# Attention followed by a squared-ReLU MLP: the second half of the attention written out in order, its side work dealt by units, high parts of early weights on GpSimd

## The chip, the core and the metric

One core of a Trainium2 chip runs the whole program. The metric is the device time of one execution in microseconds; lower is better. Engines are named as the profile names them: PE (TensorE), DVE (VectorE), ACT (ScalarE), POOL (GpSimd) and SP, whose queue issues the DMAs.

## The reference

```python
# q, k, v: (4, 8, 576, 64); bias: (576, 576) per head from positions by a small MLP
scores = q @ k.T / sqrt(64) + bias
attn = exp(scores - max); attn /= attn.sum(-1)
x = (attn @ v) as (2304, 512)
h = x @ w_in            # w_in (512, 2048)
out = max(h, 0)**2 @ w_out   # w_out (2048, 512)
```

The bias depends on head and positions alone, so it is computed once for the four batches.

## The kernel before

Attention works in units `(b, hp, ic)`: a batch, a pair of heads, and a chunk of 128 query rows; chunk 4 is the tail of 64 rows, in which both heads share one tile. `units` has 80 of them. The first 40 (`NA = 40`) run over both first batches, chunk by chunk, while the bias is computed into `area`. The last 40 run over batches 2 and 3, head pair by head pair, five chunks each; a head pair's part of `area` is free once its units are done.

A unit takes three steps. `scores(u)` (L420) multiplies q and k on PE (L438) into one score buffer `sp` in PSUM; DVE evicts it per head with bias and maximum (L444, `negm`), ACT takes the exponential and the row sums (L449); for a tail unit POOL copies 64 columns (L452). `transposes(u)` (L485) turns p on PE (L494, L497), ACT copies it to `pt` (L495, L498). `values(u)` (L501) multiplies with v on PE (L512) and DVE copies the result to `xT` (L517). The loop (L663) emits `scores(s)`, `transposes(s-2)`, `values(s-3)` in step s. After the last chunk of a head pair, `normalise` (L454) inverts the row sums on DVE (L457, L458), splits them in three bf16 parts on POOL (L461, L463), and turns them by one product (L466) that ACT copies (L468); `scale_x` (L471) spreads them on PE (L480) and multiplies `xT` on DVE (L483).

Beside the units runs side work for the MLP, which computes in split precision and by a seven-product block scheme. `scan_w` (L211) finds the largest weight of the 16 raw tiles of w_in, which arrive by `load_w` in two buffers tagged `stage`; `scale_w` (L214) makes a power of two of it. `split_in` (L224) makes eight early operands of w_in (`early`): `lead_w` (L171) takes absolute values on ACT (L176) and rebuilds float32 words from int64 halves in four DVE instructions (L179 to L182), POOL makes sums of blocks (L241 to L243), ACT writes the high part in f16 (L230), DVE the low part (L231). `x_largest` and `set_scale` scale x, `split_x` (L623) splits batch 0's x: sums on POOL (L635), high parts on ACT (L637), low parts on DVE (L638). The operands' places in `area` are `wdst` and `xs_at`; an operand can only be written where the bias is no longer read.

The order in each engine's queue is Tile's planner's: it takes program order as priority, places instructions by estimated times, and keeps the order written only for those passed to `keep_in_program_order` (score products after the first, scans, the first ACT instruction of early operands). Which step emits which side work is fixed by constants: `SC = 41` and `SN = 12` for scans, `WB`, `WS`, `LW` and the freeing of `area` for `when`, `XS`, `X1`, `XB` for x.

k and q of all eight first groups lie in one pool `kqa` (L91). At `s == NA` it is closed and a pool `kqb` with three buffers opened (L666, L667), into which `load_k` and `load_q` bring the second half's.

The MLP (L965 on) is written in order under `manual_schedule`: 40 items of `products` (L862), sums, squares, a split of g in high and low parts (L898, L899) and `down` (L954). Its first statements fetch two tiles of w_out (`first_outs`) and make their parts with `lead` and `high_out` (L789, L790), and run POOL's `sums_x` (L830) for batch 1.

## Time and profile before

| | us |
|---|---|
| median of 3 runs | 762.73 (762.21 to 762.75) |
| the profiled execution | 763.08 |
| its span, first to last instruction | 761.1 |
| PE busy | 719.4 (95%) |
| DVE busy | 554.9 (73%) |
| ACT busy | 476.3 (63%) |
| POOL busy | 170.3 (22%) |

The span is the time between the first and the last instruction of the profiled execution; 2.0 us lie around it. Busy time of PE holds the model's latency of a matmul, so back-to-back products overlap in their rows: what a product costs is read from one start to the next.

### The profile page before, as it was taken

Reading aid. Unit: us, or ns where it says so; the run is one execution under the profiler, and the core shown is the slowest. Engines: PE = TensorE matmul, PEld = TensorE weight load, DVE = VectorE, ACT = ScalarE, POOL = GpSimd, SP = SyncE. Lnnn points to the kernel's source line nnn. Section 1 sums busy time; section 2 is a strip of 40 time slices with the busy share of each in tenths; the row PEclk is TensorE's granted clock in tenths of the full one; section 3 lists DMA queues with packets and bytes.
Section 4 is the critical chain, followed back from the end, with each engine's and each line's share of the span. In section 5 each row is a group of like instructions: output and inputs, shape, how many; then the busy total and the mean of one; then the engine's idle time right before and its main releaser. Section 6 shows DMA issues by size and latency. Waiting matters only on the chain.

```text
span 761.1 us, 18188 instructions
## 1 busy us (share of the span) xinstructions
PE 719.4 (95%) x7382; PEld 579.0 (76%) x7382; DVE 554.9 (73%) x1178; ACT 476.3 (63%) x946; POOL 170.3 (22%) x281
## 2 busy tenths in 40 slices
PE   6889999999989999979998999999999999999992
PEld 6867878777757777657776888888888888888881
DVE  6689878775666677897498887878558775568651
ACT  4367787877647677878676675676566554455220
POOL 1474333331210023352114321312101112000000
PEclk7599999999999999999999999999999999999997
DMA  7620000000487622200350333332018332533100
GB/s 204 194 81 18 5 15 2 2 3 4 115 297 229 211 62 89 88 6 25 122 197 13 141 139 152 111 131 79 1 62 311 109 129 98 208 111 112 56 2 28
DMA packets 31607, 75.33 MB, mean 99 GB/s; under 512 B 5540, under 2 KB 13732, under 8 KB 30500
## 3 DMA queue, kind: packets, MB, share of 16 engines
q1 hardware_dynamic: 31524, 74.17, 28.5%
q8 instruction: 58, 0.95, 0.5%
q14 instruction: 25, 0.20, 0.1%
HBM read 55.81 MB, written 18.35 MB: 97 GB/s over the span
## 4 chain that ended last, share of the span: by engine, by line
PE 78%; DVE 11%; ACT 3%; issue 2%; DMA 2%; POOL 1%; SPq 0%; ACTq 0%; DVEq 0%
PE y L954 25%; PE ha L862 11%; PE px L512 9%; PE sp L438 9%; PE hb L862 8%; PE pp L494 7%; PE bb L386 4%; PE bb L405 2%; DVE t L444 2%; DMA stage<-in_w_in 2%; DVE mask L375 2%; PE pa L497 1%; ACT p L449 1%; DVE wa L181 1%; ACT pt L495 1%
## 5 line engine op out<-in xcount | busy, mean ns | idle before, releaser
L954 PE MATMUL y<-w,gh 128*128 128x512 f32 x576 | 183.1, 399 | 1.6 <-ACT gh L898 1.6
L862 PEld LDWEIGHTS <-area 128*128 128x128 f16 x1680 | 147.7, 98 | 25.5 <-issue 9.5
L449 ACT ACTIVATE p<-t,negm 128x576 f32<-128x576 f32 x144 | 111.1, 774 | 25.9 <-DVE negm L444 25.7
L444 DVE CUSTOM_DVE_ANT_0 t<-sp,area 128x576 f32<-128x576 f32 x144 | 103.9, 752 | 31.9 <-PE sp L438 26.9
L954 PEld LDWEIGHTS y<-w,gh 128*128 128x128 f32 x576 | 106.0, 190 | 23.3 <-ACT gh L898 2.3
L954 PE MATMUL y<-w,gl 128*128 128x512 f32 x288 | 113.9, 395 | 0.7 <-DVE gl L899 0.7
L438 PE MATMUL sp<-k,q 64*128 64x288 f32 (+1 forms) x640 | 103.0, 432 | 9.4 <-DVE negm L444 6.3
L495 ACT COPY pt<-pp 128x512 f32<-128x512 f32 x144 | 79.4, 582 | 35.4 <-PE pp L494 35.2
L512 PE MATMUL px<-pt,v 128*64 128x128 f32 (+1 forms) x1600 | 97.8, 269 | 2.8 <-DVE bt L392 1.2
L512 PEld LDWEIGHTS px<-pt,v 128*64 128x64 f32 x1600 | 80.0, 138 | 19.4 <-issue 7.6
L494 PE MATMUL pp<-ident,p 128*128 128x128 f32 x576 | 84.8, 284 | 1.6 <-ACT pt L495 1.2
L862 PE MATMUL ha<-area 128*128 128x256 f16 (+1 forms) x816 | 84.8, 260 | 0.7 <-DVE c L879 0.7
L438 PEld LDWEIGHTS sp<-k,q 64*128 64x128 f32 (+1 forms) x640 | 54.3, 177 | 31.4 <-issue 10.7
L494 PEld LDWEIGHTS pp<-ident,p 128*128 128x128 f32 x576 | 62.6, 143 | 19.2 <-issue 9.8
L397 POOL TENSOR_TENSOR area<-bt,bt 128x256 f32<-128x256 f32 x72 | 54.2, 775 | 73.2 <-DVE bt L392 73.2
L375 DVE TENSOR_TENSOR mask<-sdist,theta 128x1024 f16<-128x1024 f16 x81 | 57.2, 742 | 13.5 <-PE bb L405 7.3
L954 PEld LDWEIGHTS y<-w,gl 128*128 128x128 f32 x288 | 54.4, 189 | 13.9 <-DVE gl L899 1.9
L862 PE MATMUL hb<-area 128*128 128x256 f16 (+1 forms) x612 | 64.7, 260 | 0.0
L899 DVE TENSOR_TENSOR gl<-area,gh 128x512 fp32r<-128x512 f32 (+1 forms) x40 | 25.8, 668 | 29.8 <-ACT gh L898 28.1
L790 POOL TENSOR_TENSOR w<-wa,w 128x512 fp32r<-128x512 f32 x16 | 20.9, 1308 | 96.1 <-ACT w L789 96.1
L386 PEld LDWEIGHTS <-mask 128*128 128x128 f16 x1152 | 37.4, 100 | 4.8 <-issue 3.7
L386 PE MATMUL bb<-wmov,mask 128*128 128x64 f16 x1152 | 41.0, 197 | 0.0
(173 smaller groups left out, 980.3 us busy)
## 6 DMA issues: line engine op xcount, KB each, us to landing
stage<-in_w_in SPq DMA_DIRECT2D x24, 512.0 KB, 4.1
r<-in_w_out SPq DMA_DIRECT2D x16, 512.0 KB, 5.9
xs<-area SPq DMA_DIRECT2D x4, 1792.0 KB, 12.9
py<-o SPq DMA_DIRECT2D x12, 512.0 KB, 3.5
o<-py SPq DMA_DIRECT2D x12, 512.0 KB, 4.3
v<-in_v SPq DMA_DIRECT2D x16, 320.0 KB, 4.3
q<-in_q SPq DMA_DIRECT2D x32, 128.0 KB, 3.5
zw<-in_w_in SPq DMA_DIRECT2D x8, 512.0 KB, 3.6
```

The lines of the kernel that those rows point to most:

```text
L375: DVE.tensor_tensor(out=out, in0=win, in1=th, op=ALU.is_ge)
L386: PE.matmul(bb[:, 64 * (7 - r):64 * (8 - r)], lhsT=m[:, r], rhs=wmov[:, n], start=(n == 0), stop=(n == 1))
L397: POOL.tensor_tensor(out=dst, in0=tw, in1=sw, op=ALU.add)
L438: mm = PE.matmul(out_t[to, x, :HALF], lhsT=qt[rows, cols], rhs=kt[rows, k0:k0 + HALF], start=True, stop=True)
L444: DVE.tensor_tensor_reduce(out=t.rearrange("p (x n) -> p x n", x=2), in0=sp[:, :, :HALF], in1=bias.rearrange("p (x n) -> p x n", x=2), sca ...
L449: ACT.activation(out=p[:, S * n:S * n + S], in_=t, func=AF.Exp, bias=negm[:, n:n + 1], scale=-1.0, accum_out=sums[:, 2 * ic + n:2 * ic + n ...
L494: PE.transpose(pp[:, 128 * c:128 * c + 128], p[:, k0:k0 + 128], ident)
L495: ACT.copy(pt[:, 4 * h:4 * h + 4], pp.rearrange("p (c m) -> p c m", c=4))
L512: PE.matmul(px[64 * h:64 * h + 64, :w], lhsT=vt[:, c, h], rhs=src, start=(c == 0), stop=(c == 4))
L862: PE.matmul(h[:, s, :w], lhsT=a, rhs=x, start=(k == 0), stop=(k == 5))
L899: DVE.tensor_tensor(out=gl, in0=g, in1=gh.bitcast(F32), op=ALU.subtract)
L954: PE.matmul(y_t[n][k], lhsT=a[:, slot, o:o + 128], rhs=x, start=((n, P) in firsts and f == 0 and m == 0), stop=((n, P) in lasts and f == 1 ...
```

## The change

The loop over steps stops at the first half. The second half (s from 40 to 83) is one region under `manual_schedule`: each engine gets its instructions in the order in which they are emitted. A step emits the loads, the score products, the transposes, then in turns ACT's copies and the softmax of the two heads, then `fill(s)`, then `values(s-3)`.

Side work is kept as jobs: lists of stages, each with an engine, a price in microseconds and a function. Per step DVE gets room of 1.65 (2.5 in a tail step) and ACT of 0.45 (1.9); `fill` goes through the jobs in order and emits a stage when its time has come and its engine has room. A stage on another engine waits for the next step, except after PE and from DVE to POOL. Normalisations and scales go ahead of other jobs.

k and q of the first three groups lie in `kqa` with three buffers, which the second half uses again; those of the other five in `kqb`, closed at the end of the first half. The second half's first loads are emitted at s = 34 and 35. Raw tiles of w_in are fetched five at a time into `stage` (two), `zw` and the places of the two first outs; the scans go by room from step 41.

Early operands have their own instruction lists: `lead` in three stages, POOL's sums, the high part on POOL (`tensor_scalar`, two instructions) in place of ACT (one), the low part on DVE in two instructions in place of one. The next operand's fetch follows the low part of an earlier one; the two first outs come last, in the attention, by the same rule. In `area`, x of batch 0 now lies at 0 to 3584, the early operands from 3584 on, and the operands 7 to 11 at the start of the second half of `area`. `wa` has three buffers instead of two, `small` 72 columns instead of 128. The MLP's text loses the statements for the first outs.

```diff
-    kq_p = [kq_stack.enter_context(tc.tile_pool(name="kqa", bufs=AB * HP, side="right"))]
+    kqa = kq_stack.enter_context(tc.tile_pool(name="kqa", bufs=KB, side="right"))
+    kqb = half_stack.enter_context(tc.tile_pool(name="kqb", bufs=AB * HP - KB, side="right"))
...
+    def high_in(n, eng=ACT):
+        for src, hi, lo in parts_in(n):
+            if eng is ACT:
+                ACT.activation(out=hi, in_=src, func=AF.Identity, scale=wscale[0])
+            else:
+                eng.tensor_scalar(out=hi, in0=src, scalar1=wscale[0], scalar2=None, op0=ALU.mult)
...
-    xs_at = [take(1, o, 7 * 512) for o in (896, 6528)]
+    xs_at = [take(0, 0, 7 * 512), take(1, 6528, 7 * 512)]
...
+    def loads(s):
         for m, g in enumerate(groups[AB * HP:]):
-            if s == max(first[g] - KL, NA):
+            if s == max(first[g] - KL, NA - AB * HP + 2 + m):
                 load_k(*g)
                 load_q(*g)
...
+    def lag(a, b):
+        return int(a != b and a != "PE" and (a, b) != ("DVE", "POOL"))
...
+    def fill(s):
+        for j in list(jobs):
+            while j[1] and max(j[0], *j[1][0][3:], 0) <= s:
+                eng, cost, fn = j[1][0][:3]
+                if room.get(eng, 1) < (0.7 * cost if eng == "DVE" else 0):
+                    break
+                if eng in room:
+                    room[eng] -= cost
+                fn()
+                j[1].pop(0)
+                if j[1]:
+                    j[0] = s + lag(eng, j[1][0][0])
...
+    raws = ("stage", "stage", "zw", "w2", "w3")
+    now = [0]
+
+    def scan(k):
+        scan_w(k)
+        if k + len(raws) < NF:
+            fetch_in(ins[k + len(raws)], raws[k % len(raws)])
...
+    dest_at = [53] + [60] * 6 + [70]
+    early_raw = ("stage", "stage", "zw", "w3") * 2
+
+    def in_job(n):
+        m = early.index(n)
+        tag = early_raw[m]
+        at = dest_at[m] + 1
+        job(
+            now[0],
+            ("SP", 0, lambda: fetch_in(n, tag)),
+            ("ACT", 0.67, lambda: lead(n, 1), now[0] + 2),
+            ("DVE", 0.85, lambda: lead(n, 2)),
+            ("DVE", 1.38, lambda: lead(n, 4)),
+            ("POOL", 2.0, lambda: sums_in(n)),
+            ("POOL", 1.3, lambda: high_in(n, HI_ENG), at),
+            ("DVE", 0.48, lambda: low_in(n, (0,))),
+            ("DVE", 0.88, lambda: low_in(n, (1,))),
+            ("SP", 0, lambda: more(m)),
+        )
...
+    with tc.manual_schedule():
+        job(NA + 1, *(("DVE", 0.68, lambda k=k: scan(k)) for k in range(NF)))
+        x_job(NA + 4, 0)
+        x_job(NA + 7, 1)
+        for u in range(NA - TL - 1, NA):
+            norm_job(u)
+        for s in range(NA, NU + TL + 2):
+            now[0] = s
+            full = s < NU and units[s][2] < TAIL
+            room["DVE"] = min(room.get("DVE", 0), 0.3) + (1.65 if full else 2.5)
+            room["ACT"] = min(room.get("ACT", 0) + (0.45 if full else 1.9), 1.5)
+            loads(s)
+            if s == NA:
+                for m, tag in enumerate(raws):
+                    fetch_in(ins[m], tag)
+            if s < NU:
+                negm, sps = score_products(s, False)
+            copies = transposes(s - TL) if s - TL < NU else []
+            for n in range(2):
+                for c in copies[n:n + 1 if n == 0 else None]:
+                    ACT.copy(*c)
+                if s < NU and n < len(sps):
+                    softmax(s, n, negm, sps[n])
+            while waiting:
+                scale_x(*waiting.pop(0))
+            if s < NU and ends(s):
+                norm_job(s)
+            fill(s)
+            if s - TL - 1 < NU:
+                values(s - TL - 1)
+    assert not jobs
```

## Rows read from the trace of the kernel before

**Rows 1.** The page: busy tenths of PE in 40 slices of the span.

```profile
PE   6889999999989999979998999999999999999992
```

**Rows 2.** Windows by stage: start and end, length, busy time (instructions) by engine, clock, DMA, GB/s.

```profile
204.68:226.48 21.80, 17.87 (x174) 12.38 (x172) 13.34 (x35) 10.89 (x29) 4.48 (x12) 0.92 0.74 263
226.48:244.82 18.34, 17.80 (x192) 13.55 (x192) 13.77 (x37) 12.13 (x31) 1.22 (x6) 1.00 0.77 243
...
323.80:348.58 24.78, 19.80 (x193) 14.55 (x193) 22.81 (x48) 19.25 (x45) 12.41 (x15) 0.93 0.06 22
...
204.68:376.13 171.45, 158.00 (x1677) 115.91 (x1675) 125.96 (x324) 123.74 (x301) 42.79 (x91) 0.98 0.37 121
...
376.13:416.61 40.48, 37.56 (x244) 30.32 (x241) 33.98 (x50) 25.05 (x35) 10.52 (x8) 0.96 0.35 125
```

**Rows 3.** Timeline of PE, bias-free units of the first half: start, length, instruction.

```profile
177.10 1.31 PE L512 MATMUL px<-pt,v 128*64 128x128 f32 x20
178.34 1.09 PE L494 MATMUL pp<-ident,p 128*128 128x128 f32 x8
...
179.48 1.24 PE L438 MATMUL sp<-k,q 64*128 64x288 f32 x8
180.65 1.31 PE L512 MATMUL px<-pt,v 128*64 128x128 f32 x20
```

**Rows 4.** Timeline of PE at the attention's end: tail unit, last normalisation, first MLP product.

```profile
367.79 1.19 PE L438 MATMUL sp<-k,q 64*64 64x288 f32 x8 [0.19 <-PE pp L494]
...
372.78 0.66 PE L494 MATMUL pp<-ident,p 128*128 128x128 f32 x4
...
373.48 1.78 PE L512 MATMUL px<-pt,v 128*64 128x128 f32 x36
375.19 0.23 PE L466 MATMUL rp<-ident_b,parts 128*27 128x128 bf16 x1
...
375.76 0.41 PE L480 MATMUL ra<-rows,pick 27*64 27x128 bf16 x8
...
376.13 0.39 PE L862 MATMUL ha<-area 128*128 128x256 f16 x2
```

**Rows 5.** Waits from 204.68 to 376.13: who waited for whom, total, times, longest.

```profile
DVE small L185 <- DMA stage<-in_w_in: 8.9, 8, 3.4
...
PE sp L438 <- DVE negm L444: 6.3, 6, 3.2
```

**Rows 6.** Timeline of all engines where the second half begins: units 39 and 40.

```profile
197.07 1.24 PE L438 MATMUL sp<-k,q 64*128 64x288 f32 x8
...
198.35 0.47 SPq L133 DMA_DIRECT2D k<-in_k  x1
...
204.68 0.78 PEld L438 LDWEIGHTS sp<-k,q 64*128 64x128 f32 x6 [0.22 <-DMA q<-in_q]
```

**Rows 7.** Timeline of DVE, one unit's evictions and a copy of values.

```profile
209.77 0.76 DVE L444 CUSTOM_DVE_ANT_0 t<-sp,area 128x576 f32<-128x576 f32 x1
...
210.45 0.75 DVE L444 CUSTOM_DVE_ANT_0 t<-sp,area 128x576 f32<-128x576 f32 x1
...
211.17 0.29 DVE L517 COPY xT<-px 128x128 f32<-128x128 f32 x1
```

**Rows 8.** Groups of instructions by line: count, busy us, mean ns, idle before.

```profile
L231 DVE SCALAR_TENSOR_TENSOR area<-zw,small,area 128x896 f16<-128x896 f32 x8 | 9.2, 1149 | 3.7 <-ACT area L230 3.6
...
L242 POOL TENSOR_TENSOR zw<-zw 128x256 f32<-128x256 f32 x8 | 5.8, 730 | 0.0
...
L181 DVE SCALAR_TENSOR_TENSOR zw<-stage,zw 128x512 int32<-128x512 int32 x8 | 5.5, 690 | 0.1
...
L243 POOL TENSOR_TENSOR zw<-zw 128x128 f32<-128x128 f32 x8 | 3.6, 455 | 0.0
...
L533 POOL CAST ident_b<-ident 128x128 bf16<-128x128 f32 x1 | 0.3, 291 | 0.1
```

**Rows 9.** Timelines of POOL and DVE at 328.9 us.

```profile
328.94 1.60 POOL L830 TENSOR_TENSOR xT<-xT 128x512 f32<-128x512 f32 x1
...
329.33 1.75 DVE L181 SCALAR_TENSOR_TENSOR wa<-r,wa 128x512 int32<-128x512 int32 x1
```

More of the change, by code (lines that the diff above doesn't have):

```diff
@@ L157, in attention_then_relu2_mlp @@
     ins = [n for n in range(2 * NF) if n // 2 % 2 == 0]
-    small = keep.tile([128, 128], F32, name="small")
+    small = keep.tile([128, 72], F32, name="small")
     used = [0]
@@ L593, in take, with words, fetch, fetch_out @@
         return area[:, o:o + n]
+    def words(t):
+        return t.bitcast(I32).rearrange("p (g n t) -> p g n t", g=2, t=2)
+    def fetch(n, t):
+        src = (w_in, w_out)[n // 2 % 2][n // 4 * 2 + n % 2]
+        SP.dma_start(out=t.bitcast(I32), in_=src.bitcast(I32))
+        wraw_t[n] = words(t)
+    def fetch_out(n):
+        fetch(n, home[n].tile([128, 1024], F32, name=f"r{n}", tag=f"w{n}", bufs=1))
+    zraw = {}
+    def raw_tile(tag):
+        return stage_p["p"].tile([128, 1024], F32, name="raw", tag=tag, bufs=2 if tag == "stage" else 1)
@@ new lines, in fetch_in, with lead, copy_out @@
+    def fetch_in(n, tag="zw"):
+        zraw[n] = raw_tile(tag)
+        fetch(n, zraw[n])
+    scratch = {}
+    def lead(n, upto=7):
+        if upto & 1:
+            scratch[n] = stage_p["p"].tile([128, 2, 256], F32, name="wa", tag="wa", bufs=3)
+        lead_w(n, scratch[n].bitcast(I32), upto)
+    def copy_out(n):
+        a = scratch[n].rearrange("p g n -> p (g n)")
+        t = home[n].tile([128, 2, 512], F32R, name=f"w{n}", tag=f"w{n}", bufs=1)
+        ACT.copy(t[:, 0], a)
+        w_t[n] = t[:, 0], t[:, 1]
@@ L713, in attention_then_relu2_mlp @@
                 load_xc(chunks[n + 2])
-        if 0 <= s - TL < NU:
-            transposes(s - TL)
-        if 0 <= s - TL - 1 < NU:
-            values(s - TL - 1)
-            b, hp, ic = units[s - TL - 1]
-            if s - TL - 1 == NU - 1 or units[s - TL][:2] != (b, hp) and (b >= AB or ic == chunks[-1]):
+        if s >= TL:
+            for dst, src in transposes(s - TL):
+                ACT.copy(dst, src)
+        u = s - TL - 1
+        if u >= 0:
+            values(u)
+            b, hp, ic = units[u]
+            if ends(u):
@@ L720, in attention_then_relu2_mlp @@
                 waiting.append((b, hp, normalise(b, hp)))
-            if waiting and (len(waiting) > 1 or waiting[0][:2] != (b, hp)):
+            if waiting and waiting[0][:2] != (b, hp):
                 scale_x(*waiting.pop(0))
-        while waiting and s == NU + TL:
-            scale_x(*waiting.pop(0))
-    assert not waiting
+    prep_stack.close()
+    half_stack.close()
+    pre = ctx.enter_context(tc.tile_pool(name="pre", bufs=1, side="left", reuse_waits="tile"))
+    stage_p["p"] = pre
@@ new lines, in power_job, with product @@
+    def power_job(at, cols, then):
+        st = {}
+        def product():
+            st["pw"] = ps.tile([128, 512], F32, name="pw", tag="aux", bufs=4)
+            PE.matmul(st["pw"][:, 0:1], lhsT=ones, rhs=cols, start=True, stop=True)
+        jobs.insert(len(norms), [at, [("PE", 0, product), ("DVE", 0.9, lambda: then(st["pw"][:, 0:1]))]])
+    raws = ("stage", "stage", "zw", "w2", "w3")
[4 more added lines that the diff above has]
+            fetch_in(ins[k + len(raws)], raws[k % len(raws)])
+        if k == NF - 1:
+            jobs.insert(len(norms), [now[0] + 1, [("DVE", 0.75, lambda: power_job(now[0] + 1, top_w(), scaled))]])
+            for n in early[:3]:
+                in_job(n)
@@ new lines, in attention_then_relu2_mlp, with more, out_job @@
+    HI_ENG = POOL
+    order = list(early[3:]) + list(first_outs)
+    def more(m):
+        if order:
+            n = order.pop(0)
+            if n in early:
+                in_job(n)
+            else:
+                out_job(n)
+    def out_job(n):
+        job(
+            now[0],
+            ("SP", 0, lambda: fetch_out(n)),
+            ("ACT", 0.67, lambda: lead(n, 1), now[0] + 2),
+            ("DVE", 0.85, lambda: lead(n, 2)),
+            ("DVE", 1.38, lambda: lead(n, 4)),
+            ("ACT", 0.62, lambda: copy_out(n)),
+            ("POOL", 1.3, lambda: rest_out(n)),
+        )
@@ L971, in attention_then_relu2_mlp @@
         sums_x(*split_at[0])
-        for n in first_outs:
-            lead(n)
-            high_out(n)
         for i in range(NI + 1):
```

354 lines of the change are left out of this document (163 added, 191 removed).

## The prediction, made before the changed kernel was run

> **What bounds the kernel now.** I read the page's busy slices first: TensorE is near 9 tenths from slice 9 on, in both halves of the attention and in the MLP [rows 1]. So a gain can only come from a stretch in which TensorE is busy with breaks, or slow. The windows by stage come next [rows 2]. The second half of the attention (units 40 to 79, from the first score product of unit 40 at 204.68 us to the first MLP product at 376.13 us) takes 171.45 us, while DVE works in 126.0, ACT in 123.7 and POOL in 42.8 of them. No engine but TensorE is near its limit on the mean, yet the five units from 323.80 take 24.78 us where those from 226.48 take 18.34.
>
> What TensorE needs is read where nothing disturbs it, in the last bias-free units of the first half [rows 3]. There a step is values 1.24 (177.10 to 178.34), transposes 1.14 (to 179.48), scores 1.17 (to 180.65): 3.55 us without a hole. A tail unit needs less [rows 4]: its scores take 1.19 on the clock where a full one's take 1.24, so 1.12; its transposes 0.70 (372.78 to 373.48); 36 value products of one full and 0.8 of a tail unit take 1.71, so 0.58 for a tail. A normalisation is 0.37 of spread (375.76 to 376.13) and 0.16 of the small product before it, so 0.53. Between 204.68 and 376.13 stand 40 score groups (32 full, 8 tail), 42 of transposes (34, 8), 43 of values (35, 8) and 12 normalisations:
>
> - scores 32 x 1.17 + 8 x 1.12 = 46.4
> - transposes 34 x 1.14 + 8 x 0.70 = 44.4
> - values 35 x 1.24 + 8 x 0.58 = 48.0
> - normalisations 12 x 0.53 = 6.4
>
> Together 145.2 us. So 171.45 - 145.2 = 26.2 us are lost there. The waits name where: DVE stands 8.9 us for raw weights, and TensorE 6.3 us for DVE's evictions of the scores [rows 5]; with one score buffer, a DVE that stands holds up TensorE. In that first stretch the granted clock was 0.92 of full, so part of the time TensorE ran at the lower of its two levels, 1.2 GHz, behind such a stand [rows 2].
>
> **The change part by part.**
>
> *Places for k and q.* The second half's k and q get three buffers that are free as soon as units 32 to 34 have been multiplied, so their loads are issued at steps 34 and 35. Before, they were issued from 198.35 on, and unit 40's scores began at 204.68, behind the DMA of q: 7.6 us after unit 39's at 197.07, where a step with one normalisation needs 3.55 + 0.53 = 4.1 [rows 6]. That is 3.5 us, but TensorE did later units' work in part of them. Bounds 0 and 3.5; I take 1.5.
>
> *The scans of w_in.* 16 reductions as before, but with five raw tiles in flight instead of two, and each new fetch behind a scan five ahead of its use. The 8.9 us of DVE's waits go if the fetches keep up. Bounds 0 and 8.9 left; I take 1.0 left on TensorE, since 16 x 0.52 MB over ten steps of 3.6 us is 233 GB/s, and that first stretch already ran at 263 GB/s with loads and all [rows 2].
>
> *The dealing by units.* In emitted order each step's DVE queue is: two evictions, other work up to the step's room (1.65 us for a full unit, 2.5 for a tail one), one copy of the values. Evictions take 0.68 each from start to start and the copy 0.29 [rows 7]: 1.36 + 0.29 + 1.65 = 3.3 us in 3.55 of TensorE's. The next scores may start 2.38 us (transposes and values) after the last ones ended, and the evictions need 1.36 of that, so DVE may be about 0.8 us late before TensorE feels it. Following the rule through the steps, the costs written in the code are 8.5 to 9.4 us of DVE work in every five steps, against a room of 9.1, and nothing is left over. The scans end at step 49, the weights' scale comes at 51, the eight early operands end at steps 57, 62, 63, 67, 70, 72, 75 and 77, and the two first outs in the last steps. ACT gets 15.6 us beside 2.9 a step. TensorE's work is unchanged. So the sum per step fits; what is left is order.
>
> *High parts on GpSimd.* Eight ACTIVATEs leave ACT; POOL gets 16 tensor_scalars over 640 and 256 columns, an operation that this trace does not show. The upper bound is POOL's two-input price: 0.455 us for 128 columns and 0.730 for 256 [rows 8], so 2.15 ns a column, and 2 x 0.18 + 896 x 0.00215 = 2.3 us for the pair. The lower is the one-input cast, 0.291 for 128 columns [rows 8], less the same 0.18: 0.9 ns a column, 1.15 us. I take 1.2, since a tensor_scalar also has one input from memory. (The Trainium skill, "GPSIMD Engine Reference", section 4.1, says that one-input work there is roughly at line rate and two-input work about twice as slow; by it the lower end holds.) DVE's low part becomes two instructions, 1.36 by the code's prices for one of 1.149 [rows 8]: 8 x 0.2 = 1.7 us more of DVE, inside the room.
>
> *The new wait.* For operands 3 to 7 the sums and the high part are dealt in the same step as the last lead instruction, and DVE's low part in the next. POOL needs 0.73 + 0.73 + 0.455 + 1.2 = 3.1 us for them [rows 8]; DVE comes to the low part after one copy and two evictions, 1.65 us. So DVE stands 1.4 us there, and behind it in its queue wait the copy of values and the next step's evictions, hence TensorE. Less the 0.8 of slack that is 0.6 x 5 = 3.0 us. Bounds: 0 if spare time before the evictions swallows it, 5 x 1.4 = 7 if there is no slack, 12 at POOL's higher price.
>
> *DVE beside POOL.* A shift-and-mask of two SBUF inputs takes 0.69 us alone and took 1.75 while POOL added [rows 8, 9]. Such pairs meet in the second half now as well, so only the increase and the cluster at steps 59 to 62 count (POOL then has 8.5 us queued over 10.6, DVE six such instructions): 6 x 0.5 us, half of it on the path, 1.5. Bounds 0 and 14 (worked out below).
>
> *Raggedness.* The best five steps of before took 18.34 us with TensorE busy for 17.80; the sum for five is 4 x 3.55 + 2.4 + 0.53 = 17.1. I leave 0.4 in each five, 3.0 in all; bounds 0 and 8 x 1.2 = 9.6.
>
> *The MLP.* Its head (376.13 to 416.61, 40.48 us [rows 2]) had the leads of the first outs and two of its sums done earlier already: the MLP's sum of line 830 stands at 328.94, amid the attention [rows 9]. The outs are now dealt there by hand; the two sums go back to the head, where ACT has other tiles first. I count 0, bounds -1.5 and +1.5. Weights and x operands only trade addresses.
>
> The sum: 26.2 + 1.5 = 27.7 to be had; left behind 1.0 + 3.0 + 1.5 + 3.0 = 8.5; gain 19.2 us. The profiled execution took 763.08 us (its span 761.1 and 2.0 around it), so 743.9; the median of the runs is 0.35 lower, so 743.5.
>
> **The rivals.**
>
> *The shared port decides.* After step 53 DVE has about 59 instructions with two SBUF inputs or of the fast scalar kind, and POOL reads SBUF for 8 x 3.1 + 5 x 1.3 + 2 x 1.3 = 34 us of some 100. If a third of them meet POOL and lose 0.7 each (at most 1.06 by the row), that is 14 us, and if TensorE feels all of it: 3.0 + 14 + 1.0 + 3.0 = 21 left behind, gain 6.7, 756 us. For it speaks the cluster at 328 to 331 us [rows 9], which belongs to the slowest five steps [rows 2]; against it that POOL is mostly dealt work just before evictions, which read PSUM. (The Trainium skill, "SBUF — State Buffer", section "Who interferes with whom", says that such a DVE instruction and a POOL instruction that reads SBUF exclude each other for their whole length. The 1.75 against 0.69 agrees, and the page speaks against giving POOL more.) Chance 0.15.
>
> *The fetches still come late.* The raw tiles lie where first-half tiles lay, and 233 GB/s beside k, q and v is close to what was moved. Then the 8.9 us stay in DVE's queue and 7 of them on TensorE: 750 us. Chance 0.10.
>
> *POOL holds DVE's queue in every early operand.* In emitted order nothing steps round a low part that waits. At the higher price, and with POOL itself held by DVE (a sum of line 830 took 1.60 us [rows 9], the line's usual 128 x 512 by the slope above is 1.28), POOL needs (1.92 + 2.3) x 1.25 = 5.3 us an operand and DVE stands 3.5: eight times 28, with 1.0 + 3.0 left elsewhere 32 us, 4.3 over the 27.7: 767 us, slower. It turns slower when a stand reaches 24 / 8 = 3 us. Chance 0.08.
>
> *The order isn't what bounds.* If the planner's order was as good as the data allow, gains and losses cancel: 763 us. Chance 0.02. On the other side, everything hidden: 738 or less, 0.05.
>
> **How the numbers follow.** The forecast, 743.5 (738 to 750), has 0.60; it is the likeliest, so the predicted time. The range 737 to 758 takes in the forecast, the late fetches and most of the port's case, some 0.83. Differences under 0.2% (1.5 us) can't be told from no change here. Faster: 0.60 + 0.05 + 0.10 + 0.14 = 0.89; same 0.02 + 0.01; slower 0.08.
>
> **What would show it.** Right: unit 40's scores about 4 us after unit 39's; no DVE wait for raw weights; five steps in 17.5 to 18.5 us up to step 55 and in 18 to 19 after it; the first MLP product 150 to 155 us after unit 40's scores; POOL's pair at 1.1 to 1.3 us, and a DVE wait of 1 to 1.5 us before each low part of operands 3 to 7. Wrong: a pair over 2 us, shift-and-masks at 1.5 us in most steps, evictions waiting on ACT's exponentials, or a first half that itself takes another time; the sum takes it as it is.

## The result and the profile after

The changed kernel takes 767.82 us (median; 766.51 to 769.24), the one before 762.75 on the same chip: a ratio of 1.0056, 95% interval 1.0038 to 1.0074. It is slower by 0.6%, where 743.5 (737 to 758) was forecast. The profiled execution has a span of 765.2 us (before 761.1).

The page's busy tenths of PE and the granted clock in 40 slices of the span, to be set beside [rows 1]:

```profile
PE   6889999999989899889898999999999999999992
PEclk7599999999999999898999999999999999999997
```

Past the first three slices, those below 9 tenths inside the attention, two of them before, are five now, and in two (from 306 and from 344 us) the granted clock is lower. The windows by stage say more (start and end, length, busy time and instructions by engine, clock, DMA share, GB/s); they are units 40 to 44, 45 to 49, 65 to 69, 70 to 74, the last units with the end, the MLP's head, and the whole region from unit 40's scores to the first MLP product, as in [rows 2]:

```profile
200.74:228.80 28.06, 24.77 (x301) 18.83 (x300) 17.87 (x51) 16.71 (x46) 3.11 (x16) 1.00 0.44 155
228.80:246.98 18.18, 17.43 (x195) 13.02 (x193) 15.04 (x39) 12.76 (x34) 1.22 (x7) 1.00 0.82 266
...
305.44:329.01 23.57, 20.41 (x194) 14.96 (x192) 16.67 (x41) 14.84 (x38) 9.43 (x15) 0.86 0.35 121
329.01:352.74 23.73, 20.59 (x194) 15.20 (x193) 16.49 (x40) 14.08 (x37) 11.21 (x17) 0.86 0.01 2
352.74:380.42 27.68, 24.70 (x280) 19.01 (x278) 18.79 (x47) 17.44 (x44) 14.67 (x23) 0.94 0.17 53
380.42:420.90 40.48, 37.59 (x259) 30.66 (x256) 33.99 (x50) 25.10 (x35) 10.84 (x9) 1.00 0.34 128
...
200.74:380.42 179.68, 161.23 (x1736) 121.01 (x1735) 132.12 (x346) 119.43 (x303) 64.12 (x112) 0.95 0.32 106
```

Units 45 to 49 take 18.18 us, within the forecast's 17.5 to 18.5. Units 65 to 74 take 47.3 us at a granted clock of 0.86, so in part of them TensorE ran at 1.2 GHz. The MLP's head takes 40.48 us, exactly as before. All that matters lies between unit 40's scores and the first MLP product.

TensorE's timeline at units 39 and 40, beside [rows 6], shows the first part of the change doing what it says:

```profile
197.56 1.24 PE L421 MATMUL sp<-k,q 64*128 64x288 f32 x8
...
200.74 0.51 PE L421 MATMUL sp<-k,q 64*128 64x288 f32 x2
```

Unit 40's scores follow unit 39's after 3.2 us instead of 7.6. They now stand ahead of one first-half unit's transposes, two units' values and a normalisation (TensorE's instructions in the region go from 1677 to 1736), some 4.2 us of work that stood in front of them before. So kernels are compared here from unit 36's scores: before 189.56 us from there to the first MLP product, after 193.36.

The waits from 200.74 to 380.42 (who waited for whom; us in total, times, longest), beside [rows 5]:

```profile
PE px L520 <- DVE xT L487: 9.1, 9, 1.7
DVE area L670 <- POOL area L666: 7.3, 8, 1.3
PE rt L481 <- DVE xT L525: 2.6, 3, 1.2
PE sp L421 <- DVE negm L431: 0.8, 2, 0.5
DVE small L187 <- DMA raw<-in_w_in: 0.3, 1, 0.3
```

The two waits of before are gone: DVE's for raw weights (8.9 to 0.3) and the scores' for DVE's evictions (6.3 to 0.8). In their place DVE stands 7.3 us for GpSimd's high parts, and the value product 9.1 us for DVE's multiplication of the attention output by the spread inverse sums (L487, in `times_rows`).

The two groups of GpSimd's high parts and DVE's low parts (count, busy us, mean ns, idle before), beside [rows 8]:

```profile
L666 POOL TENSOR_SCALAR area<-raw,small 128x640 f16<-128x640 f32 x8 | 15.1, 1892 | 0.0
...
L666 POOL TENSOR_SCALAR area<-wa,small 128x256 f16<-128x256 f32 x8 | 8.0, 1003 | 0.0
...
L670 DVE SCALAR_TENSOR_TENSOR area<-raw,small,area 128x640 f16<-128x640 f32 x8 | 7.9, 994 | 3.6 <-POOL area L666 3.6
...
L670 DVE SCALAR_TENSOR_TENSOR area<-wa,small,area 128x256 f16<-128x256 f32 x8 | 5.9, 734 | 3.7 <-POOL area L666 3.7
```

A pair takes 2.9 us; 1.2 was taken and 2.3 was the upper bound. How that reaches TensorE is read in the timeline of units 67 to 69, all engines (start, length, instruction; in brackets the idle time before and its releaser):

```profile
315.72 0.92 POOL L666 TENSOR_SCALAR area<-wa,small 128x256 f16<-128x256 f32 x1
...
316.63 1.88 POOL L666 TENSOR_SCALAR area<-raw,small 128x640 f16<-128x640 f32 x1
316.68 1.02 DVE L670 SCALAR_TENSOR_TENSOR area<-wa,small,area 128x256 f16<-128x256 f32 x1 [1.30 <-POOL area L666]
...
318.54 0.89 DVE L670 SCALAR_TENSOR_TENSOR area<-raw,small,area 128x640 f16<-128x640 f32 x1 [0.85 <-POOL area L666]
319.35 0.22 DVE L525 COPY xT<-px 128x64 f32<-128x64 f32 x1
319.48 0.75 DVE L431 CUSTOM_DVE_ANT_0 t<-sp,area 128x576 f32<-128x576 f32 x1
...
319.61 0.21 PE L481 MATMUL rt<-rows,pick 27*64 27x64 bf16 x2 [1.22 <-DVE xT L525]
...
320.15 0.75 DVE L431 CUSTOM_DVE_ANT_0 t<-sp,area 128x576 f32<-128x576 f32 x1
...
320.83 0.68 DVE L487 TENSOR_TENSOR xT<-xT,ra 128x512 f32<-128x512 f32 x1
...
321.43 0.21 DVE L487 TENSOR_TENSOR xT<-xT,rt 128x64 f32<-128x64 f32 x1
...
321.57 2.40 PE L520 MATMUL px<-pt,v 128*64 128x128 f32 x20 [1.74 <-DVE xT L487]
...
323.90 1.71 PE L421 MATMUL sp<-k,q 64*64 64x288 f32 x6
```

DVE stands 1.30 and 0.85 us for the two high parts. Behind them in its queue stand the copy of values, two evictions and then the multiplication. The transposes, the values, the normalisation's product and both spread results take turns in four PSUM buffers (tag "aux"). So the next value product must wait until the multiplication has read `ra`, and the spread itself until DVE has copied an older value product out. TensorE waits 1.22 and 1.74 us, and the value product right behind takes 2.40 us instead of the 1.31 of [rows 3]: it runs at the lower clock. Unit 68's step takes 8.47 us, those of 73 and 78 take 7.96 each, and the steps right behind 68 and 73 take 5.11 and 5.27; most other steps from unit 64 on take 3.1 to 3.7.

### The profile page after: what moved, and what is told of

It is laid out like the page before. It is cut to its first block, busy times and chain, and to the rows that moved or that the text cites. A ratio compares the mean times of both kernels' runs of the same rounds, so it can differ in the third digit from the quotient of the medians.

```text
span 765.2 us, 18196 instructions
## 1 busy us (share of the span) xinstructions
PE 717.0 (94%) x7382; PEld 579.4 (76%) x7382; DVE 556.8 (73%) x1186; ACT 468.6 (61%) x938; POOL 190.3 (25%) x297
## 5 line engine op out<-in xcount | busy, mean ns | idle before, releaser
L436 ACT ACTIVATE p<-t,negm 128x576 f32<-128x576 f32 x144 | 111.7, 777 | 17.5 <-DVE negm L431 17.3
L520 PE MATMUL px<-pt,v 128*64 128x128 f32 (+1 forms) x1600 | 100.1, 273 | 13.6 <-DVE xT L487 9.1
L520 PEld LDWEIGHTS px<-pt,v 128*64 128x64 f32 x1600 | 82.0, 140 | 27.6 <-DVE xT L487 10.1
L501 PEld LDWEIGHTS pp<-ident,p 128*128 128x128 f32 x576 | 62.8, 143 | 23.0 <-issue 17.5
L934 ACT COPY pt<-pp 128x512 f32<-128x512 f32 x76 | 43.9, 579 | 46.8 <-PE pp L501 46.8
L767 ACT COPY pt<-pp 128x512 f32<-128x512 f32 x68 | 37.6, 587 | 14.1 <-PE pp L501 14.0
L652 POOL TENSOR_TENSOR raw<-wa 128x256 f32<-128x256 f32 x16 | 12.1, 754 | 119.5 <-issue 65.8
```

Source lines behind the costliest of these rows:

```text
L436: ACT.activation(out=p[:, S * n:S * n + S], in_=t, func=AF.Exp, bias=negm[:, n:n + 1], scale=-1.0, accum_out=sums[:, 2 * ic + n:2 * ic + n ...
L501: PE.transpose(pp[:, 128 * c:128 * c + 128], p[:, k0:k0 + 128], ident)
L520: PE.matmul(px[64 * h:64 * h + 64, :w], lhsT=vt[:, c, h], rhs=src, start=(c == 0), stop=(c == 4))
L767: ACT.copy(dst, src)
L934: ACT.copy(*c)
```

## The experiments

All but e4 are edits of the changed kernel; the later ones build on one another. Each ratio is to the kernel before run beside it on the same chip. The summary first (e8 was made for durations alone and isn't in it): the region is from unit 36's scores to the first MLP product in the profile (1,877 or 1,878 matmuls in each), its length split into PE idle and PE busy; the busy time grows where the clock is low.

| run | median us | ratio, 95% interval | region | PE idle | PE busy | clock |
|---|---|---|---|---|---|---|
| before | 762.75 | 1 | 189.56 | 13.9 | 175.7 | 0.98 |
| after | 767.82 | 1.0056 (1.0038–1.0074) | 193.36 | 18.8 | 174.6 | 0.96 |
| e1 | 761.19 | 0.9971 (0.9952–0.9991) | 188.48 | 16.7 | 171.8 | 0.97 |
| e2 | 762.77 | 0.9993 (0.9974–1.0012) | 189.32 | 19.5 | 169.9 | 0.98 |
| e3 | 755.76 | 0.9895 (0.9871–0.9918) | 180.73 | 13.2 | 167.5 | 1.00 |
| e4 | 758.97 | 0.9936 (0.9918–0.9953) | 184.24 | 10.3 | 174.0 | 0.99 |
| e5 | 757.55 | 0.9919 (0.9902–0.9936) | 184.03 | 12.2 | 171.8 | 0.97 |
| e6 | 762.63 | 0.9984 (0.9972–0.9996) | 189.92 | 17.6 | 172.3 | 0.97 |
| e7 | 759.68 | 0.9947 (0.9929–0.9965) | 186.74 | 14.7 | 172.1 | 0.97 |
| e9 | 755.92 | 0.9908 (0.9894–0.9922) | 182.02 | 13.4 | 168.7 | 0.99 |
| e10 | 752.94 | 0.9866 (0.9853–0.9880) | 176.89 | 7.5 | 169.4 | 0.98 |
| e11 | 754.51 | 0.9894 (0.9879–0.9910) | 178.14 | 10.9 | 167.2 | 1.00 |
| e12 | 749.86 | 0.9828 (0.9814–0.9841) | 176.11 | 7.7 | 168.4 | 0.99 |
| e13 | 751.41 | 0.9855 (0.9833–0.9877) | 177.50 | 8.6 | 169.0 | 0.99 |
| e14 | 746.84 | 0.9786 (0.9764–0.9808) | 173.08 | 6.5 | 166.6 | 1.00 |

**e1, the spread earlier in its step.** The spread and the multiplication are emitted at the head of the same step, ahead of its scores, so the multiplication no longer stands behind the evictions.

```diff
-            ("ACT", 0.24, lambda: st.update(rows=norm_copy(st["rp"]))),
-            ("PE", 0, lambda: st.update(r=spread_rows(st["rows"])), u + TL + 2),
-            ("DVE", 0.9, lambda: times_rows(b, hp, *st["r"])),
+            ("ACT", 0.24, lambda: due.append((max(u + TL + 2, now[0] + 1), b, hp, norm_copy(st["rp"])))),
...
+            spread_due(s)
             if s < NU:
                 negm, sps = score_products(s, False)
```

(`spread_due` calls `scale_x` for each entry whose step has come.)

> The changed kernel, but the spread of a normalisation's rows (TensorE) and the multiplication of xT by them (DVE) are emitted at the head of a step, ahead of the score products, instead of in the fill behind the evictions. Theory A, the ring: in a step with a spread six tiles go through the four 'aux' buffers of PSUM, so the values wait until DVE has multiplied xT, and that stands behind two evictions in DVE's queue. Then the 13 us of TensorE's waits on DVE's copy and multiplication go to under 4, the stretches at half clock behind them go too, and the time is 749 to 754. Theory B, GpSimd: DVE stands 7.3 us for GpSimd's high parts and everything behind it only shows where; then the wait moves to the scores waiting for evictions and the time is 762 to 767. Theory C, emitted order as such costs: no change, 767.

Measured: 761.19 us, 0.9971. The value product's wait for the multiplication fell from 9.1 to 0.7 us, but a new one took its place (e1's waits of TensorE):

```profile
PE ra L481 <- ACT rows L464: 11.3, 8, 1.7
```

ScalarE's copy of the rows stands behind the exponentials of the step before. DVE still stands 8.2 us for GpSimd. The time is none of the three expected: the tie to the multiplication is real, and this place trades it for another queue.

**e2, the high parts back on ScalarE, same places.**

```diff
-    HI_ENG = POOL
+    HI_ENG = ACT
```

> The changed kernel with one part undone: the high parts of the eight early operands are written by ScalarE again (two ACTIVATEs, 0.5 and 0.8 us), emitted at the same places; GpSimd does the sums only. Theory A, the ring: the values still wait for the multiplication of xT (9 us now; 4 to 6 when DVE comes to it earlier), 759 to 764. Theory B, GpSimd's high parts (2.9 us a pair) are the cause: DVE's 7.3 us of waits go to under 2 and the loss goes, 748 to 754. Theory D, ScalarE then stands for the sums as DVE did: the exponentials come late and the time is 764 to 770.

Measured: 762.77 us, 0.9993. Its waits:

```profile
PE px L520 <- ACT pt L934: 12.5, 9, 3.0
ACT area L664 <- POOL raw L654: 7.6, 6, 1.5
PE px L520 <- DVE xT L487: 4.3, 6, 0.8
```

Now ScalarE stands for GpSimd's sums at the head of its queue, and its copies of the transposed weights come late, as theory D said; the time is theory A's. Only 5 us come back: what costs is an in-order engine standing behind GpSimd, whichever engine it is.

**e3, the low parts one step later.** DVE comes to the low part when GpSimd is done; whatever follows the low part, the next fetch above all, moves with it.

```diff
     def lag(a, b):
+        if (a, b) == ("POOL", "DVE"):
+            return 2
         return int(a != b and a != "PE" and (a, b) != ("DVE", "POOL"))
```

> The changed kernel, but DVE's low parts are dealt two steps after GpSimd's high parts instead of one; the high parts stay on GpSimd. Theory B, the stand of DVE for GpSimd: 7.3 us of waits go to under 1 and the time is 750 to 756, as without GpSimd's high parts. Theory A, the ring: half of TensorE's waits stay, since the multiplication still stands behind the evictions, 758 to 763. If the port that DVE and GpSimd share costs, rather than the wait, the low parts take over 1 us in many places and the time stays at 765 to 768.

Measured: 755.76 us, 0.9895. The stand is gone, 12 us come back, though the last interval is 2.2 us longer, and the clock is 1.00 over the whole region. The time is theory B's. Of the tie this is left:

```profile
PE px L520 <- DVE xT L487: 5.6, 8, 1.1
```

The spread steps take 4.69 to 5.26 us, most of them 4.74; most steps beside them 3.1 to 3.6.

**e4, the kernel before with the new places of k and q alone.**

```diff
-            if s == max(first[g] - KL, NA):
+            if s == max(first[g] - KL, NA - AB * HP + 2 + m):
```

with the pool of three buffers for it (`KB = 3`).

> The kernel before with one part of the change alone: k and q of the first three groups in three buffers that the second half uses again, its first loads emitted at steps 34 and 35. By the step of the prediction: unit 40's scores begin 3 to 4 us after unit 39's instead of 7.6, and 0 to 3.5 us are gained, 1.5 taken: 759.5 to 762.5. Rival: what TensorE gains there it had done ahead otherwise, no change, 762.7.

Measured: 758.97 us, 0.9936, so 3.6 to 6.3 us gained where 1.5 was taken and 3.5 was the bound. Unit 40's scores begin 3.19 us after unit 39's, and a window of the same length from there as units 40 to 44 had before (in [rows 2]: 21.80 us, 174 matmuls, clock 0.92; it ends 0.5 us short of unit 45's scores) now reads:

```profile
201.42:223.11 21.69, 20.69 (x233) 14.96 (x233) 16.52 (x46) 13.96 (x39) 5.43 (x17) 1.00 0.65 208
```

In the same time 59 more matmuls are done. But it was not the wait for q that cost the time. In the kernel before, TensorE worked in 7.16 of the 7.61 us between the scores of units 39 and 40, at the full clock (its window), and what stopped it came 11 us later (its timelines of DVE and PE):

```profile
197.07:204.68 7.61, 7.16 (x88) 5.49 (x88) 5.21 (x16) 5.28 (x16) 1.97 (x10) 1.00 0.51 138
...
215.86 0.69 DVE L185 TENSOR_REDUCE small<-stage 128x1 f32<-128x512 f32 x1 [3.38 <-DMA stage<-in_w_in]
...
218.55 2.18 PE L438 MATMUL sp<-k,q 64*128 64x288 f32 x8 [3.19 <-DVE negm L444]
```

There a scan stood for its raw weights, the evictions behind it, and the scores behind those; after that TensorE ran at the lower clock. In e4 this stand doesn't come: DVE's waits for raw weights are 3.6 us instead of 8.9, the scores' for evictions 2.7 instead of 6.3. From unit 39's scores to unit 42's the kernel before takes 14.51 us and e4 14.15; from there to unit 45's 14.90 and 11.23. Why the raw tiles are there in time in e4 isn't shown.

**e5 and e6, the spread a whole step later, with and without e3's edit.** The rows then have a step for ScalarE's copy (`min(u + TL + 3, NU + TL + 1)` in e1's edit). e5 has e3's edit too, e6 hasn't.

> The changed kernel with two edits: the low parts of the early operands are emitted two steps behind GpSimd's high parts instead of one place behind (as in the run with that edit alone, 755.8 us), and the spread of the inverse sums together with VectorE's multiplication moves to the head of the step after, ahead of that step's scores, a whole step after ScalarE's copy of the rows. Theory ring (the four-buffer PSUM ring ties the value product to VectorE's multiplication, which stands behind the evictions): the run with the first edit alone still had eight spread steps of 4.74 us against 3.5 and 5.6 us of waits of the value product for the multiplication; these go, 5 to 9 us: 747 to 751 us, spread steps at or under 3.8 us. Rival (the multiplication only gets a new partner to wait for, as ScalarE's copy of the rows in the run with the spread at the head of its own step): 753 to 757 us.

> The changed kernel with the second edit alone: spread and multiplication at the head of the step after, a whole step after ScalarE's copy of the rows; the low parts stay where they are, so VectorE still stands for GpSimd's high parts. Theory ring (that stand of 2 to 3 us reaches TensorE only through the multiplication queued behind it): with the multiplication ahead of the stand most of the loss goes, 750 to 755 us. Rival (the stand reaches TensorE through the evictions of the next scores too, since one score buffer leaves little slack): 757 to 763 us, with new waits of the scores for VectorE's evictions of over 3 us in sum.

Measured: e5 757.55 us, e6 762.63. In e5 the spread steps 48, 58, 68, 73 and 78 take 3.94 to 4.03 us against 4.74 to 5.14 in e3, as the tie foretold; yet the kernel is slower than e3, because the last interval, from unit 79's scores to the first MLP product, grew from 11.53 to 17.18 us (9.38 in the changed kernel). e5's waits name it:

```profile
ACT wa L178 <- DMA r<-in_w_out: 7.3, 1, 7.3
```

ScalarE stood for a freshly fetched output operand, its copies of the last transposed weights queued behind. The dealing counts steps, and at the end steps are short. e6 shows that DVE's stand costs its time with the multiplication out of the way too: then TensorE waits for ScalarE's copies (5.4, 3.3 and 2.8 us) and DVE stands 10.1 us; units 68 to 70 and 73 to 75 take 6.1 us more together than in e5. Theory ring, as written for e6 (that the stand reaches TensorE only through the multiplication), fell. The time is the rival's, but the waits on its path, of the scores for the evictions, are only 1.5 us. The way goes on from the evictions through ScalarE's queue, as e6's timeline shows: an exponential waits for an eviction, and the copy of transposed weights for which the spread waits stands behind it.

```profile
319.60 0.77 ACT L436 ACTIVATE p<-t,negm 128x576 f32<-128x576 f32 x1 [1.72 <-DVE negm L431]
...
320.99 0.21 PE L481 MATMUL rt<-rows,pick 27*64 27x64 bf16 x2 [1.40 <-ACT pt L941]
```

**e7, the high parts on ScalarE, one step after the sums, the low parts one step after that.**

```diff
-            ("POOL", 2.0, lambda: sums_in(n)),
-            ("POOL", 1.3, lambda: high_in(n, HI_ENG), at),
+            ("POOL", 2.0, lambda: sums_in(n), at),
+            ("LATER", 0, lambda: high_in(n, ACT)),
```

> The changed kernel with the high parts on ScalarE, as before the change, but emitted one step after GpSimd's sums, and the low parts one step after that, so that no engine stands at the head of its queue for another; spread and multiplication stay. Theory stand (what cost the time was that an engine stands in order behind GpSimd, on whichever engine the high parts are): as the run with the low parts later, 754 to 759 us. Rival (the high parts take ScalarE's time beside the copies of the transposed weights, 8 x 1.2 us, and GpSimd is the better place for them): 760 to 764 us.

Measured: 759.68 us, 0.9947, between the two. It isn't decided here; e13 does it better.

**e8, four forms of the high part on GpSimd** (for their durations alone, in e3's order).

> The disputed price by itself: the changed kernel with the low parts two steps later, and the high parts on GpSimd in four forms, two operands each: a plain copy, a multiplication by a constant in the instruction, an addition of the source to itself, and the multiplication by a scalar in SBUF as in the change (so the values of six operands are not scaled rightly). Measured: the time of the 640-column instruction. Theory scalar (the scalar read from SBUF makes it slow): 1.89 us for that form, 1.0 to 1.4 us for the other three. Rival (one source with a rounded output runs at 2.9 ns a column whatever the form): 1.8 to 1.9 us for all but the addition, and 1.4 us for that by the 2.15 ns a column of GpSimd's sums. The time of the kernel itself is as the run with that edit alone, 754 to 757 us.

GpSimd's groups of 640 columns:

```profile
L674 POOL TENSOR_SCALAR area<-raw,small 128x640 f16<-128x640 f32 x2 | 4.1, 2035 | 0.0
...
L670 POOL TENSOR_SCALAR area<-raw 128x640 f16<-128x640 f32 x2 | 3.6, 1807 | 0.0
...
L672 POOL TENSOR_TENSOR area<-raw 128x640 f16<-128x640 f32 x2 | 2.7, 1346 | 0.0
...
L668 POOL CAST area<-raw 128x640 f16<-128x640 f32 x2 | 1.9, 953 | 0.0
```

The scalar in SBUF isn't the cause: with a constant it is 1.81 us. Nor is one source with a rounded output: the two copies took 0.72 and 1.18 us, the longer one beside a low part on DVE. The multiplication by a scalar is the slow operation, 2.8 to 3.2 ns a column, slower than adding two sources (2.1 on the mean) and over twice the shorter copy (1.1). Both theories fell.

**e9, the high parts by the copy**, in the changed kernel's own order.

```diff
-                eng.tensor_scalar(out=hi, in0=src, scalar1=wscale[0], scalar2=None, op0=ALU.mult)
+                eng.tensor_copy(out=hi, in_=src)
```

> The changed kernel with one edit: GpSimd makes the high parts by a plain copy instead of the multiplication by a scalar, same places, same queue order (it leaves out the scale of the high parts of eight operands). In the run with four forms a copy of 640 columns took 0.95 us and one of 256 columns 0.40, so a pair costs 1.35 us, near the 1.2 on which the prediction rests, against 2.9 in the changed kernel. If the price of the pair is the failing step of the prediction, the time comes to 744 to 752 us. If the failing step is rather the queue (VectorE's multiplication, and behind it the value product, waits for whatever GpSimd still has to do, its sums of 1.92 us first), the stand is only 1.5 us shorter in each of eight operands and 755 to 763 us are left.

Measured: 755.92 us, 0.9908. GpSimd's high parts:

```profile
L666 POOL CAST area<-raw 128x640 f16<-128x640 f32 x8 | 6.2, 781 | 0.0
...
L666 POOL CAST area<-wa 128x256 f16<-128x256 f32 x8 | 3.7, 457 | 0.0
```

With the pair at 1.24 us, the price of the forecast, DVE stands 1.8 us in all instead of 7.3, and 11 to 12 us come back, but not the other 12: the time lies at the lower edge of what was expected if the queue failed rather than the price. DVE's low parts take 1.00 and 0.68 us on the mean here, about as in the changed kernel (0.99 and 0.73), so it isn't their stretching beside GpSimd that the 12 us were lost to.

**e10 and e11, the last operand's first step behind the region**, on e5 and on e3.

```diff
-            ("ACT", 0.67, lambda: lead(n, 1), now[0] + 2),
+            ("ACT", 0.67, lambda: lead(n, 1), max(now[0] + 2, NU + TL + 1)),
```

> The run with low parts, spread and multiplication later (757.6 us), with one edit more: the first step of the late output operands, which ScalarE does on freshly fetched weights, is emitted behind the last step of the region (the loop over the steps runs on for four steps without scores). In the run without it ScalarE stood 7.3 us there for the fetch, with the copies of the transposed weights of the last two units behind it, and the last interval was 17.18 us against 9.4 in the changed kernel. Theory (the two edits work in every step, and the end hid it): 748 to 751 us. Rival (the stand only moves: the first MLP items wait for that operand, or for VectorE, which makes it): 753 to 758 us.

> The run with the low parts later alone (755.8 us) with the same edit at the end: there ScalarE stood 3.2 us for the fetch, and the last interval was 11.53 us. Theory: 752 to 754 us, so that the run with spread and multiplication later as well, beside this one on the same chip, is faster by 2 to 6 us, which is what the PSUM ring alone costs. Rival (the multiplication's place costs nothing once VectorE doesn't stand): both within 1 us of each other.

Measured: e10 752.94, e11 754.51 us. The last interval is 9.07 in both, but 2.4 us of it come back in the MLP (first product to item 5: 53.0 us against 50.6), where TensorE waits for the operand, as e10's rival said (its time is 753 or more); e10's waits show it:

```profile
PE ha L1001 <- ACT w L633: 3.1, 1, 3.1
```

Between the two the spread's place is worth 1.6 us in the medians (the intervals touch), less than the 2 to 6 expected: 0.7 to 1.1 us a spread step saved, but steps 53, 63 and 64 grew by 5.0 together.

**e12, the same end by another way:** the two output operands are fetched into raw buffers one operand sooner (on e5).

```diff
-        fetch(n, home[n].tile([128, 1024], F32, name=f"r{n}", tag=f"w{n}", bufs=1))
+        fetch(n, raw_tile("stage") if n in first_outs else home[n].tile([128, 1024], F32, name=f"r{n}", tag=f"w{n}", bufs=1))
...
     def more(m):
-        if order:
+        for _ in range(2 if m == 4 else 1):
+            if not order:
+                break
```

> The run with low parts, spread and multiplication later (757.6 us), with another cure for its end: the two late output operands are fetched into the two raw buffers of the early operands 4 and 5, one operand sooner, so their first step on ScalarE is dealt sooner and finds its data. In the run that moved this step behind the region (752.9 us) the first MLP items took 2.4 us longer (53.0 from the first product to item 5, against 50.6). Theory: neither wait is left, last interval 9 to 10 us, first MLP items 50.6, time 749 to 751.5 us. Rival (VectorE's three steps of that operand, dealt into the last units, hold up the evictions there as much as was saved): 752 to 756 us.

> The run before this one with the high parts on ScalarE, emitted one step after GpSimd's sums, and the low parts one step after that. Theory order (the high parts cost nothing on either engine once nobody stands for them, so this part of the change is neither good nor bad in itself): within 1.5 us of the run before. Rival (GpSimd relieves ScalarE of 8 x 1.15 us, and ScalarE's copies of the transposed weights come later without it): 2 to 6 us slower than the run before.

Measured: e12 749.86 us, last interval 9.39, first MLP items 50.45, as its theory said. e13, e12 with e7's edit, takes 751.41, a difference of 1.6 with intervals that touch, between its two expectations: once nobody stands for them, no difference is shown between the high parts on one engine and on the other.

**e14, ScalarE's high parts of the x operand also two steps behind GpSimd.** In e12 steps 63 and 64 still take 6.92 and 5.06 us. Its timeline of POOL, ACT and PE there:

```profile
294.62 1.88 POOL L666 TENSOR_SCALAR area<-raw,small 128x640 f16<-128x640 f32 x1
296.47 3.07 POOL L708 TENSOR_TENSOR raw<-xT 128x512 f32<-128x512 f32 x2
...
297.77 0.72 ACT L714 ACTIVATE area<-raw,small 128x512 f16<-128x512 f32 x1 [2.95 <-POOL raw L708]
...
299.62 0.41 PE L481 MATMUL ra<-rows,pick 27*64 27x128 bf16 x8 [2.71 <-ACT pt L945]
```

```diff
-        if (a, b) == ("POOL", "DVE"):
+        if (a, b) in (("POOL", "DVE"), ("POOL", "ACT")):
             return 2
```

> The run with the outs fetched sooner (749.9 us), and ScalarE's high parts of the x operand emitted two steps behind GpSimd's sums instead of one. Theory (steps 63 and 64, 6.92 and 5.06 us, are long because ScalarE stands 2.95 us for a sum that GpSimd, with four high parts queued ahead of it, hasn't begun): the two steps come to 7 to 9 us together and the time to 745 to 747.5 us. Rival (GpSimd's backlog itself, and what its long instructions do to VectorE's beside them, moves the delay into other steps): 748.5 to 751 us.

Measured: 746.84 us, 0.9786, as its theory said; steps 63 and 64 take 4.91 and 3.49. Its windows of units 65 to 69 and 70 to 74, where the changed kernel needed 23.57 and 23.73 us:

```profile
300.85:318.89 18.04, 17.51 (x194) 13.05 (x192) 16.66 (x40) 15.16 (x38) 10.79 (x15) 1.00 0.45 157
318.89:337.23 18.34, 17.58 (x194) 13.05 (x192) 15.84 (x38) 14.44 (x37) 14.10 (x18) 1.00 0.16 54
```

The same 194 matmuls are busy for 17.5 us instead of 20.5, and TensorE is idle for 0.5 and 0.8 instead of 3.2 and 3.1. This is the fastest kernel of the study: the change as it is, with every step of DVE and ScalarE that follows GpSimd one step later, spread and multiplication a step later, and the late fetches sooner.

## Why the prediction was wrong

The 24 us between forecast and result come apart in three: 12 for DVE's stand behind GpSimd (gone in e3 by order, in e9 by price, so the two steps that follow are factors of one loss and don't add), 9 for other places of the order (e3 to e14), and 3 that are left.

**The price of GpSimd's pair failed.** "I take 1.2", between 1.15 and 2.3, was 2.9 us, so "a pair over 2 us" among the signs of being wrong came true. Both bounds came from other operations (a cast, a two-input sum), on the assumption that a multiplication by a scalar lies between them; e8 shows it above both. The Trainium skill, "GPSIMD Engine Reference", section 4.1, whose one-input rate spoke for the lower end, is borne out by the copy (0.72 us for 640 columns where nothing stretched it; DVE's low part of as many takes 0.88) and not by this operation. By e9 a pair at the price taken would have saved 11 to 12 us.

**"Less the 0.8 of slack" failed, and with it which of DVE's products TensorE waits for.** The sum asked only when the evictions come, since there is one score buffer. For them the slack was there: the scores waited 0.8 us in all. But the value product and the spread wait, through the four aux buffers, for the copy and the multiplication, which come last in DVE's queue; those have no slack. Nor does the slack of the scores cover ScalarE: with the multiplication out of the way (e6) late evictions hold up the exponentials, and the copies behind them hold up TensorE. In total DVE stood 7.3 us, and that this is near the 7.0 that the forecast had before it took the slack off is luck: at the measured price the same rule gives 5 x (1.4 + 1.7) = 15.5, and at the price that it took DVE stood 1.8 (e9). What failed is what such a stand costs: e3, where it is gone, is 12 us faster. More than half of these 12 us is TensorE working slower: from the changed kernel to e3 its idle time falls by 5.5 us and its busy time, for the same matmuls, by 7.1, while the granted clock goes from 0.96 to 1.00. The sum had no term for TensorE working slower behind a wait, though [rows 2] showed it (0.92 and 0.93).

**The new order has two more stands that the sum left at nothing.** ScalarE stands for the x operand's sum on GpSimd (e14 against e12, 3.0 us in the medians), and, once the operands are dealt later, for the last fetch (e5). "The sum per step fits; what is left is order" was right, and the order was then taken as good. Its price is the way from the changed kernel to e14, 21 us in the medians, with all the instructions kept.

**The places for k and q** were undersized, and for a wrong reason: 1.5 taken, 3.6 to 6.3 measured (e4), above the upper bound. Of the 3.5 us that the forecast read as a wait for q, TensorE stood 0.45; it did later units' work in nearly all of the rest. What e4 gives back is a stand for raw weights 11 us later and the lower clock behind it, which the sum had under the scans: two of its terms share one gain.

**Right:** the scans (1.0 left taken; DVE's waits for raw weights are down to 0.3 us), and the MLP at 0 (40.48 us in both). DVE beside POOL, 1.5 taken: DVE's low parts took 0.99 and 0.73 us, against 0.88 and 0.48 where GpSimd is idle (e14 at 310.26 us, e3 at 318.02 us), 8 x (0.11 + 0.25) = 2.9 us of DVE, part of it in the same stands; its shift-and-masks kept 0.69. The shared port didn't decide: e9's low parts are as long, and its 12 us came back. Nor does a high part of 1.88 us on GpSimd keep a low part out for its whole length, as the port's rival in the prediction has it: the one that starts 0.05 us into it, at 316.68 us, takes 1.02 us, and the one that starts 0.98 us into it, at 332.70 us, 0.43.

**Raggedness**, 3.0 (bounds 0 and 9.6), can be read only in e14: 6.5 us of idle TensorE from unit 36 on, four first-half units included. The forecast amounts to a region of 189.56 - 19.2 = 170.4 us from unit 36; e14 has 173.08. So what was to be had was about right, 746.84 against 743.5, but the change as written doesn't collect it.

**The rivals.** "POOL holds DVE's queue in every early operand" (0.08) gave 767 us and is what happened in kind, but that its time came out right is luck: it had DVE stand 28 us, and 7.3 were measured. Its point of decision was wrong: it turned slower not at a stand of 3 us an operand but at 7.3 / 8 = 0.9 on the mean, because a stand shortly before a spread step costs TensorE the wait and then, as far as the order in time shows, the clock. Since the pair's price had no row of its own, that rival deserved far more, and the price's upper end should have lain above both neighbours. The late fetches (0.10) didn't come.

What stays open: that the clock falls because of these waits is argued from their order in time (1.31 becomes 2.40 us right behind one); no run changed the clock alone, and e5 and e7, without DVE's stand, still show 0.97 in the region, e5 with its last 17 us at 0.80 around ScalarE's stand. In e1 and e6 it isn't shown which of several waits let the clock fall. Which of the four aux buffers a product takes isn't in the trace either: that the value product waits for the multiplication's read is taken from the times at which the two end and begin (321.51 and 321.57 us) and from e1.

## What to carry to other kernels

In an order that is emitted by hand, a step that follows another engine's work belongs where that work is surely done: cost a wait by everything queued behind it on its engine, and follow each of those through every ring of buffers to TensorE, not only through the nearest one. An operation that the trace doesn't show on an engine can cost more than each of its neighbours there; the range must say so, and a single run with its forms settles it. Budgets in units say that a step's work fits, not that it arrives in time; at the end of a region, where steps shorten, a distance counted in steps shrinks.

## What was not expected of the hardware

- On GpSimd a multiplication by a scalar, f32 to f16, takes 1.81 to 2.04 us for 640 columns, with the scalar in the instruction or in SBUF (e8 and the changed kernel); adding two sources takes 1.25 and 1.44 (e8), and a copy 0.72 to 0.74, or 1.18 once in each of e8 and e9 beside a low part on DVE.
- A low part of 256 columns on DVE that starts 0.05 us into such a multiplication of 1.88 us takes 1.02 us, one that starts 0.98 us into it 0.43 (the changed kernel at 316.68 and 332.70 us), against 0.48 with GpSimd idle (e3 at 318.02 us); GpSimd's instruction doesn't get longer.
- 7.3 us of standing on DVE, with no wait of TensorE over 1.74 us, went along with 7.1 us of longer matmuls in the region, at a granted clock of 0.96 instead of 1.00 (the changed kernel against e3).
